# One core, pooled attention into a squared-ReLU layer into a soft mixture of experts: a later v pooling, a conversion step on another engine, and reloads in eight parts

## The chip, the cores and the metric

One core of a Trainium2 chip runs the whole program. The metric is the device time in microseconds (us) of one execution, the median of several. The kernel before takes 785.67 us (three runs, 785.44 to 789.61). A difference of about 0.5% (4 us) is what a measurement of this kernel can tell from no change.

The engines are named as in the profile: PE is TensorE's matmul side and PEld its weight loads, DVE is VectorE, ACT is ScalarE, POOL is GpSimd, SP is the engine from whose queue (SPq) every DMA of this kernel is issued.

## The reference

All inputs are drawn in float64 or float32 and the output is float32 of 4608 x 512. Cut to what is computed:

```
# attention: 8 sequences, 8 heads, 576 tokens, head size 64; k and v are averaged over groups of 8 tokens
k_p = k.reshape(B, H, Sp, 8, D).mean(axis=3);  v_p = v.reshape(B, H, Sp, 8, D).mean(axis=3)
attn = softmax(q @ k_p^T / sqrt(D));  x = attn @ v_p            # as 4608 x 512
# layer: d_ff 2048
g = max(x @ w_in, 0) ** 2;  y = g @ w_out
# soft mixture: 8 experts, 4 slots each
logits = y @ phi
d = softmax over tokens(logits);  slot_input = d.T @ y
slot_out[e] = max(slot_input[e] @ w1[e], 0) @ w2[e]
out = softmax over slots(logits) @ slot_out
```

## The kernel before

The 4608 tokens are 36 tiles of 128 (`t` = 0 to 35). For each tile the attention steps (`att_qT` to `att_av`) give x as two parts, `xh` and `xl`, whose sum keeps float32 precision. The first layer runs in **units**: unit (t, j) multiplies the tile's x with quarter j of `w_in` (512 of the 2048 columns) in 12 matmuls on PE into one of two PSUM buffers `l1` (line 453). There are 144 units, numbered here 0 to 143 in the order in which they run; from unit 16 on they go by pairs of tiles, (4,0) (5,0) (4,1) (5,1) and so on. ACT takes the ReLU of a finished unit (`r`, line 466), and the square `g` is made by DVE (line 473) or ACT (line 475). For the units of tiles 0 to 5 ACT squares; from unit 24 on, the first of tile 6, six of eight squares are DVE's. A PSUM buffer is free for the unit after next only when the square that reads it is done. Each g (256 KB) is stored to `g_dram` (line 477).

`w_out` is never multiplied with g in full: `phi` is folded into it (`turn_wo`, `fold_phi`, `sum_a`), which gives a small matrix `a_sb`. Its four quarters are loaded as float64 (`load_w`, line 373, 4 x 512 KB each, into the two buffers st0 and st1 in turn) and turned into float32 in integer and float steps by `f32_steps`: one on ACT (line 342), three on DVE (344, 347, 351), one addition on the engine that is handed in or else on GpSimd (355), one on DVE (356). `conv_out` (line 405) calls this for each of 16 pieces, with no engine handed in.

For a pair of tiles the logits need g transposed: `reload_turned` reads 512 KB of it back from `g_dram` in a transposing pattern (line 506, into `turned` or `tmp`), DVE finishes the transpose in blocks (`g_T`, line 514), PE multiplies with `a_sb` (`logits`, line 539), then `log_T` (568 on), `d_T` (603) and `dg` (613) add the pair's softmax-weighted g to the slot inputs. `dg` needs g itself. For the late pairs (from tile 10 on) it is still in SBUF; for the five **early pairs** (t = 0, 2, 4, 6, 8) `reload_g` reads the pair's 2 MB back into one buffer `g_back` (tag st0, lines 493 to 499) with two DMAs of 1 MB.

k and v of each sequence b are loaded in four parts of 288 KB (line 150) into three buffers `kv` that k and v share, and pooled. For the third sequence (b = 2) k is pooled by PE (`pool_k`, line 164, then 171 on DVE and 174 on ACT) and v by four DVE reductions of two heads each (`pool_v_dve`, line 189). They are called v0 to v3 here. From b = 3 on GpSimd pools (lines 157 to 159).

Order: the loop over the units runs each unit in two halves, called **slots** (slot 2u and 2u+1), and `at(slot, fn, ...)` hangs further work on a slot; `pinned(name, fn, ...)` hangs it behind the last instruction that was noted under a name, for instance the last store. The framework then orders each engine's instructions by a timeline that it simulates, so a slot is a wish and not a place. Each engine, and SP's queue, works through its own order strictly: an instruction that waits holds up all behind it.

Of the kernel before, what the change touches and what calls it, by code (L numbers as in the profile page):

```python
# [8 lines left out]
F32 = mybir.dt.float32  # L9
# [8 lines left out]
def kernel(  # L18
# [12 lines left out]
    nc = tc.nc  # L31
# [8 lines left out]
    P = 128  # L40
# [3 lines left out]
    NQ = 4  # L44
    QF = DFF // NQ
# [17 lines left out]
    stp = ctx.enter_context(tc.tile_pool(name="stp", bufs=1))  # L63
# [10 lines left out]
    vpp = (kvp, a3)  # L74
# [12 lines left out]
    g_dram = [dram.tile([2, NQ, CPQ, P, P], F32, tag=f"g_dram{t}", name=f"g_dram{t}") for t in range(0, NT - 4, 2)]  # L87
# [243 lines left out]
    def to_f32(src, dst=None, eng=None):  # L331
        steps = f32_steps(src, dst, eng)
        for _ in range(3):
            dst = next(steps)
        return dst

    def f32_steps(src, dst=None, eng=None):
        hi, lo = src[:, :, 1], src[:, :, 0]
        val, mag, low = (tmp[:, (3 * n_conv[0] + i) % 8] for i in range(3))
        n_conv[0] += 1  # L340
        dst = mag if dst is None else dst
        nc.scalar.activation(out=val, in_=hi.bitcast(F32), func=AF.Copy, scale=2.0 ** -112)  # L342
        yield
        nc.vector.tensor_scalar(  # L344
            out=mag.bitcast(U32), in0=val.bitcast(U32), scalar1=3, scalar2=None, op0=ALU.logical_shift_left
        )
        nc.vector.tensor_scalar(
            out=low.bitcast(U32), in0=val.bitcast(U32), scalar1=3, scalar2=0x7F800000,
            op0=ALU.logical_shift_left, op1=ALU.bitwise_and,
        )  # L350
        nc.vector.scalar_tensor_tensor(  # L351
            out=low, in0=lo, scalar=2.0 ** -52, in1=low, op0=ALU.mult, op1=ALU.mult
        )
        yield
        (eng or nc.gpsimd).tensor_tensor(out=mag, in0=mag, in1=low, op=ALU.add)  # L355
        nc.vector.scalar_tensor_tensor(
            out=dst.bitcast(U32), in0=val.bitcast(U32), scalar=0x80000000, in1=mag.bitcast(U32),
            op0=ALU.bitwise_and, op1=ALU.bitwise_or,
        )
        yield dst  # L360
# [38 lines left out]
    wo_t = {}  # L399

    def conv_out(j, c):
        st = st_t["out", j]
        if c == 0:
            wo_t[j] = st.rearrange("p c d two -> p c (d two)").bitcast(F32)[:, :, :DM]
        to_f32(st[:, c], wo_t[j][:, c])

    def natural(x):
        return x.rearrange("p (a c f) -> p c a f", a=4, f=32)
# [31 lines left out]
    hp_t, g_t, gT_t, L_t, dT_t, d_t, sc_d = {}, {}, {}, {}, {}, {}, {}  # L440
# [39 lines left out]
            if t >= ND:  # L480
                g_t[t, j] = g

    xbuf, gT_at = [], {}
    gT_free = [1, 2, 3, 4, 5]

    def turned():
# [4 lines left out]
        return xbuf  # L491

    def reload_g(t):
        g = stp.tile([P, 2, NQ, QF], F32, tag="st0", name="g_back")
        for u in range(2):
            nc.sync.dma_start(
                out=g[:, u].rearrange("p j (c f) -> p (j c) f", f=P),
                in_=g_dram[t // 2][u].rearrange("j c p f -> p (j c) f"),
            )
            for j in range(NQ):  # L500
                g_t[t + u, j] = g[:, u, j]

    def reload_turned(t, j):
        i = gT_at[t, j] = gT_free.pop(0)
# [242 lines left out]
    def at(slot, fn, *a):  # L747
        ev.setdefault(slot, []).append((fn, a))
# [20 lines left out]
    def post(t, s0, o, step=4):  # L769
        for j in range(NQ):  # L770
            if t < ND:
                at(s0 + step * j + o[1], pinned, "logits", logits, t, j)
            else:
                at(s0 + step * j + o[1], logits, t, j)
        for j in range(NQ):
            at(s0 + step * j + o[0], pinned, "sq", g_T, t, j)
            at(s0 + step * j + o[2], pinned, "store", reload_turned, t, j)

    def post_end(t, s0, p):
        at(s0 + p[0], log_T, t)  # L780
        at(s0 + p[1], d_T, t)
        if ND <= t < NT - 8:
            at(s0 + p[2], behind_l1, dg, t)
        else:
            at(s0 + p[2], dg, t)
# [42 lines left out]
    for j in range(NQ):  # L828
        s0 = 26 + 12 * j
        at((17, 31, s0 - 8, s0 - 8)[j], load_w, "out", j)  # L830
        for c in range(CPQ):
            at(s0 + 3 * c, paced, conv_out, j, c)
        at(s0 + 13, store_wo, j)
        for kk in range(KD):
            at(s0 + 14 + kk, behind_l1, turn_wo, j, kk)
        at(s0 + 22, behind_l1, fold_phi, j)
        at(s0 + 25, behind_l1, sum_a, j)
# [11 lines left out]
    for t in (NT - 4, NT - 2):  # L849
        s0 = SLOTS * t  # L850
# [12 lines left out]
    at(266, lambda: behind([("w1", 0, 1)], load_tail, 2))  # L863
    for t in range(0, ND, 2):
        s0 = 96 + 28 * (t // 2)
        at(s0 - 5, reload_g, t)
        post(t, s0, (3, 6, -2), 4)
        post_end(t, s0, (20, 21, 23))
    for b in range(1, B):
        s0 = a_at[b * S // P]  # L870
        for i in range(NPAIR):
            at(s0 - 16 + 2 * i, load_kv, k, raw_k, b, i)
            if b in PEP:
                at(s0 - 12 + 2 * i, pool_k, b, i)
            else:
                at(s0 - 12 + 2 * i, pool_kv, nc.gpsimd, raw_k, kp_t, b, i, kvp, "kp")
            at(s0 - 10 + 2 * i, load_kv, v, raw_v, b, i)
            if b in PEP:
                at(s0 - 4 + 2 * i, pool_v_dve, b, i, vpp[b % 2])
            else:  # L880
                at(s0 - 4 + 2 * i, pool_kv, nc.gpsimd, raw_v, vp_t, b, i, vpp[b % 2], "vp")
        if b not in PEP:
            at(s0 - 4, make_kb, b)
# [269 lines left out]
```

## Time and profile before

| | us |
|---|---|
| median of three runs | 785.67 |
| profiled execution, its own time | 786.77 |
| its span, first to last instruction | 785.0 |
| PE busy in the span | 732.8 (93%) |
| DVE busy | 517.2 (66%) |
| ACT busy | 392.7 (50%) |
| POOL busy | 149.1 (19%) |
| mean granted TensorE clock | 0.969 of full |

All times below are microseconds from the span's start in that execution. The units of the first layer run from 35 to 700; before that inputs arrive and are pooled, after it the experts and the output follow. The granted clock is a share of full speed: 1.00 is the 2.4 GHz level, 0.50 the 1.2 GHz one.

### The profile page before, as it was taken

To read this page: it belongs to the slowest core of one execution; us is meant where nothing else is said; L and a number is where in the kernel's file an instruction comes from. 1 tells how busy PE (TensorE), PEld (TensorE's weight loads), DVE (VectorE), ACT (ScalarE), POOL (GpSimd) and SP (SyncE) were. 2 spreads that over 40 slices of the span, in tenths; PEclk is the share of its full clock that TensorE was granted. 3 is DMA by queue.
4 is the path that set the end of the run, shared out by engine and by line. 5 is a ranking of instruction groups with operands and counts; after the bars stand their busy time and mean duration, and the time that the engine had idled before them with its cause. 6 is when DMAs were issued, how large, how long until landed. Compare 5 with 4: busy or idle time off the path is not lost.

```text
span 785.0 us, 14474 instructions
## 1 busy us (share of the span) xinstructions
PE 732.8 (93%) x5260; PEld 514.5 (66%) x5260; DVE 517.2 (66%) x1033; ACT 392.7 (50%) x1135; POOL 149.1 (19%) x167
## 2 busy tenths in 40 slices
PE   8789999979899999998999997989998999998993
PEld 7667787767677767575667664656665766663462
DVE  2996855485736678788868857868796765324253
ACT  2675677444547464444736551637385444332142
POOL 2232311164633500171022301320000000000000
PEclk7799999989999999999999999999999999999997
DMA  8955854758585884995696678769576325979998
GB/s 263 307 162 169 250 148 134 226 156 261 132 264 149 249 230 142 281 277 135 185 295 195 181 224 253 199 215 239 156 211 231 121 81 219 416 254 333 374 310 296
DMA packets 208296, 175.11 MB, mean 223 GB/s; under 512 B 74592, under 2 KB 165728, under 8 KB 208224
## 3 DMA queue, kind: packets, MB, share of 16 engines
q1 hardware_dynamic: 208224, 174.17, 72.2%
q8 instruction: 42, 0.69, 0.4%
q14 instruction: 30, 0.25, 0.1%
HBM read 126.94 MB, written 47.19 MB: 222 GB/s over the span
## 4 chain that ended last, share of the span: by engine, by line
PE 64%; DMA 10%; DVE 10%; ACT 5%; SPq 4%; POOL 3%; issue 2%; ACTq 0%; POOLq 0%; DVEq 0%
PE l L453 38%; PE misc L613 3%; PE pl L539 3%; DMA kv<-in_v_dram 2%; PE misc L1074 2%; DMA kv<-in_k_dram 2%; ACT aT L284 2%; PE l L1042 2%; PE gT L311 2%; PE gT L234 2%; DMA tmp<-g_dram 2%; PE att L234 2%; POOL kv L157 2%; PE att L311 2%; SPq L131 1%
## 5 line engine op out<-in xcount | busy, mean ns | idle before, releaser
L453 PE MATMUL l<-w,xh 128*128 128x512 f32 x1152 | 386.7, 415 | 10.1 <-DVE g L473 5.4
L453 PEld LDWEIGHTS l<-w,xh 128*128 128x128 f32 x1152 | 210.4, 192 | 85.3 <-issue 20.1
L453 PE MATMUL l<-w,xl 128*128 128x512 f32 x576 | 231.3, 402 | 0.0
L466 ACT ACTIVATE r<-l 128x512 f32<-128x512 f32 x144 | 86.6, 602 | 177.9 <-PE l L453 166.5
L453 PEld LDWEIGHTS l<-w,xl 128*128 128x128 f32 x576 | 110.0, 191 | 28.8 <-issue 3.5
L284 ACT COPY aT<-turned 32x256 f32<-32x256 f32 (+1 forms) x168 | 67.8, 403 | 23.3 <-DVE turned L293 19.7
L157 POOL TENSOR_TENSOR kv<-kv 72x512 f32<-72x512 f32 x40 | 55.0, 1379 | 125.7 <-DMA kv<-in_v_dram 78.8
L473 DVE TENSOR_TENSOR g<-l,r 128x512 f32<-128x512 f32 x57 | 38.8, 681 | 27.1 <-ACT r L466 21.0
L514 DVE STREAM_TRANSPOSE turned<-turned 128x1024 f32<-128x1024 f32 x39 | 47.5, 1227 | 10.8 <-DMA turned<-g_dram 10.8
L245 ACT ACTIVATE es<-gT,mx 128x72 f32<-128x72 f32 x120 | 36.8, 328 | 21.6 <-DVE mx L241 21.6
L245 ACT ACTIVATE es<-att,mx 128x72 f32<-128x72 f32 x120 | 37.0, 336 | 8.1 <-DVE mx L241 7.9
L286 DVE COPY aT<-turned 32x256 f32<-32x256 f32 (+1 forms) x120 | 37.2, 310 | 1.7 <-PE gT L311 0.2
L396 POOL TENSOR_TENSOR w<-tmp,w 128x512 fp32r<-128x512 f32 x16 | 22.8, 1430 | 70.1 <-ACT w L395 61.9
L473 DVE TENSOR_TENSOR tmp<-l,r 128x512 f32<-128x512 f32 x33 | 22.5, 682 | 18.7 <-ACT r L466 10.7
L475 ACT ACTIVATE g<-r 128x512 f32<-128x512 f32 x54 | 34.3, 636 | 0.9
L514 DVE STREAM_TRANSPOSE tmp<-tmp 128x1024 f32<-128x1024 f32 x25 | 30.4, 1226 | 6.2 <-DMA tmp<-g_dram 6.2
L355 POOL TENSOR_TENSOR tmp<-tmp 128x512 f32<-128x512 f32 x16 | 20.5, 1283 | 59.1 <-DVE tmp L351 59.1
L158 POOL TENSOR_TENSOR kv<-kv 72x256 f32<-72x256 f32 x40 | 30.6, 774 | 0.8
L613 PE MATMUL misc<-g,d 128*32 128x512 f32 x134 | 25.1, 620 | 5.1 <-DVE d L603 4.2
L268 DVE TENSOR_TENSOR es<-es,rs 128x576 f32<-128x576 f32 x36 | 28.8, 799 | 0.8
L344 DVE TENSOR_SCALAR tmp<-tmp 128x512 uint32<-128x512 uint32 x32 | 15.6, 488 | 19.8 <-ACT tmp L342 19.8
L159 POOL TENSOR_TENSOR kp<-kv 72x128 f32<-72x128 f32 x20 | 9.4, 484 | 100.6 <-PE att L204 100.6
(195 smaller groups left out, 1094.5 us busy)
## 6 DMA issues: line engine op xcount, KB each, us to landing
g_dram<-g SPq DMA_DIRECT2D x95, 256.0 KB
turned<-g_dram SPq DMA_DIRECT2D x39, 512.0 KB
w<-in_moe_w_dram SPq DMA_DIRECT2D x32, 512.0 KB
tmp<-g_dram SPq DMA_DIRECT2D x25, 512.0 KB
w<-in_moe_w_dram SPq DMA_DIRECT2D x6, 2048.0 KB
kv<-in_k_dram SPq DMA_DIRECT2D x32, 288.0 KB
kv<-in_v_dram SPq DMA_DIRECT2D x32, 288.0 KB
out_dram<-o SPq DMA_DIRECT2D x36, 256.0 KB
```

Source lines behind the costliest of these rows:

```text
L157: eng.tensor_tensor(out=x[:, :, 0:4], in0=x[:, :, 0:4], in1=x[:, :, 4:8], op=ALU.add)
L234: mark["sc", t] = nc.tensor.matmul(sc[off:off + n, i * 2 * SP:(i + 1) * 2 * SP], qT[:, pi, off:off + n], kb[b % 2][:, pi].rearrange("p a s ...
L245: mark["es", t] = nc.scalar.activation(out=es[:, e], in_=sv[:, h], func=AF.Exp, bias=mx[:, e:e + 1], accum_out=rsum[:, t % 8, e, 0:1],)
L284: nc.scalar.copy(out=dst, in_=src)
L286: eng[e].tensor_copy(dst, src)
L311: nc.tensor.matmul(px[e * D:(e + 1) * D, i * P + off:i * P + off + n], vp_t[b][:, 2 * i + e], aT[:, 2 * i + e, off:off + n],)
L453: mm = mark["l1", t, j] = nc.tensor.matmul(hp_t[t, j], steps[i][0], steps[i][1], start=(i == 0), stop=(i == 2 * n - 1))
L466: nc.scalar.activation(out=r, in_=hp, func=AF.Relu, scale=1.0 / (R * R if sq == "V" else R))
L473: mark["sq"] = nc.vector.tensor_tensor(out=dst, in0=pre, in1=src, op=ALU.mult)
L475: nc.scalar.activation(out=dst, in_=src, func=AF.Square)
L514: nc.vector.transpose(out=gc.rearrange("p (n i) -> p n i", i=32), in_=gc.rearrange("p (n f) -> p n f", f=32))
L613: mark["dg"] = nc.tensor.matmul(dp[32 * j:32 * j + 32], d[:, u], g if t < NT - 4 else natural(g), start=(u == 0), stop=(u == width(t) - 1),)
```

## The change

Three edits. The conversion of `w_out` is handed `nc.vector`, so its addition (line 355) goes from GpSimd to DVE, 16 times. The reload of an early pair's g is cut into eight DMAs of 256 KB, each behind the last store, one every three slots from three slots ahead of the pair's first slot to 18 slots behind it; the buffer is claimed one slot before. The DVE pooling of v is asked for `2 * b - 2` slots later: nothing for b = 1, two slots for b = 2.

```diff
-        to_f32(st[:, c], wo_t[j][:, c])
+        to_f32(st[:, c], wo_t[j][:, c], nc.vector)
...
     def reload_g(t):
-        g = stp.tile([P, 2, NQ, QF], F32, tag="st0", name="g_back")
+        g_back[t] = stp.tile([P, 2, NQ, QF], F32, tag="st0", name="g_back")
         for u in range(2):
-            nc.sync.dma_start(
-                out=g[:, u].rearrange("p j (c f) -> p (j c) f", f=P),
-                in_=g_dram[t // 2][u].rearrange("j c p f -> p (j c) f"),
-            )
             for j in range(NQ):
-                g_t[t + u, j] = g[:, u, j]
+                g_t[t + u, j] = g_back[t][:, u, j]
+
+    def reload_part(t, u, j):
+        nc.sync.dma_start(
+            out=g_back[t][:, u, j].rearrange("p (c f) -> p c f", f=P),
+            in_=g_dram[t // 2][u, j].rearrange("c p f -> p c f"),
+        )
...
         s0 = 96 + 28 * (t // 2)
-        at(s0 - 5, reload_g, t)
+        at(s0 - 4, reload_g, t)
+        for n in range(2 * NQ):
+            at(s0 - 3 + 3 * n, pinned, "store", reload_part, t, n // NQ, n % NQ)
...
             if b in PEP:
-                at(s0 - 4 + 2 * i, pool_v_dve, b, i, vpp[b % 2])
+                at(s0 - 4 + 2 * b - 2 + 2 * i, pool_v_dve, b, i, vpp[b % 2])
```

The order that comes out is the same up to unit 19. It differs at three places that matter here; line numbers of the changed kernel are up to four higher.

**Place A**, SP's queue around unit 22. `kv<-in_v` are the loads of v0 to v3, `st<-in_moe_w_out` is the third quarter of `w_out`. Before:

```order
L150 DMA kv<-in_v_dram 72x2x512
L150 DMA kv<-in_k_dram 72x2x512
L150 DMA kv<-in_v_dram 72x2x512
L477 DMA g_dram_105<-g 128x4x128
L373 DMA st<-in_moe_w_out_dram 128x1024 x4
L477 DMA g_dram_105<-g 128x4x128
L150 DMA kv<-in_v_dram 72x2x512 x2
L150 DMA kv<-in_k_dram 72x2x512
```

The same stretch of SP's queue in the changed kernel:

```order
L150 DMA kv<-in_v_dram 72x2x512
L150 DMA kv<-in_k_dram 72x2x512
L373 DMA st<-in_moe_w_out_dram 128x1024 x4
L477 DMA g_dram_105<-g 128x4x128
L150 DMA kv<-in_v_dram 72x2x512
L477 DMA g_dram_105<-g 128x4x128
L150 DMA kv<-in_v_dram 72x2x512
L477 DMA g_dram_105<-g 128x4x128
```

The 2 MB of `w_out` now stand ahead of the loads of v1, v2 and v3 (the last follows right behind these rows), where v1 was ahead of them.

DVE at the same place, from the reduction of v0 to the first square of tile 6 (`g<-l_1589`, unit 24). Before:

```order
L189 TENSOR_REDUCE vp<-kv 72x128
L319 TENSOR_TENSOR xl<-att,xh 128x512
L189 TENSOR_REDUCE vp<-kv 72x128
L171 TENSOR_SCALAR kb_119<-att 64x72 x2
L344 TENSOR_SCALAR tmp<-tmp 128x512
L347 TENSOR_SCALAR tmp<-tmp 128x512
L351 SCALAR_TENSOR_TENSOR tmp<-st,tmp 128x512
L428 COPY at_sb<-misc 128x4x4x32
L189 TENSOR_REDUCE vp<-kv 72x128
L356 SCALAR_TENSOR_TENSOR st<-tmp 128x512
L189 TENSOR_REDUCE vp<-kv 72x128
L473 TENSOR_TENSOR g<-l_1589,r 128x512
```

DVE there in the changed kernel, where unit 24 reads `l_1587`:

```order
L319 TENSOR_TENSOR xl<-att,xh 128x512
L171 TENSOR_SCALAR kb_119<-att 64x72
L344 TENSOR_SCALAR tmp<-tmp 128x512
L347 TENSOR_SCALAR tmp<-tmp 128x512
L171 TENSOR_SCALAR kb_119<-att 64x72
L189 TENSOR_REDUCE vp<-kv 72x128
L351 SCALAR_TENSOR_TENSOR tmp<-st,tmp 128x512
L189 TENSOR_REDUCE vp<-kv 72x128
L428 COPY at_sb<-misc 128x4x4x32
L355 TENSOR_TENSOR tmp<-tmp 128x512
L189 TENSOR_REDUCE vp<-kv 72x128
L473 TENSOR_TENSOR g<-l_1587,r 128x512
```

v1's reduction went behind the two `kb` rows and two conversion steps, v2's behind line 351; all four still stand ahead of unit 24's square, and the addition of line 355 is now among them.

**Place D**, DVE around the squares of units 33 and 34 (`l_2006` and `l_2077`). Before:

```order
L473 TENSOR_TENSOR g<-l_2006,r 128x512
L266 TENSOR_REDUCE rs<-rsum 128x8
L267 RECIPROCAL rs<-rs 128x8
L266 TENSOR_REDUCE rs<-rsum 128x8
L268 TENSOR_TENSOR es_121<-es_121,rs 128x576
L267 RECIPROCAL rs<-rs 128x8
L356 SCALAR_TENSOR_TENSOR st<-tmp 128x512
L268 TENSOR_TENSOR es_122<-es_122,rs 128x576
L473 TENSOR_TENSOR g<-l_2077,r 128x512
```

And in the changed kernel:

```order
L473 TENSOR_TENSOR g<-l_2006,r 128x512
L355 TENSOR_TENSOR tmp<-tmp 128x512
L266 TENSOR_REDUCE rs<-rsum 128x8 x2
L356 SCALAR_TENSOR_TENSOR st<-tmp 128x512
L267 RECIPROCAL rs<-rs 128x8 x2
L268 TENSOR_TENSOR es_121<-es_121,rs 128x576
L268 TENSOR_TENSOR es_122<-es_122,rs 128x576
L473 TENSOR_TENSOR g<-l_2077,r 128x512
```

Line 355 is now DVE's own, directly ahead of line 356 that needs it.

**Place F**, SP's queue around unit 93, where the reload of pair 6 begins (`g_dram_106` holds pair 6, `g_dram_114` the pair being computed, tiles 22 and 23). Before:

```order
L131 DMA qt<-in_q_dram 32x8x32 x2
L496 DMA g_back<-g_dram_106 128x16x128 x2
L477 DMA g_dram_114<-g 128x4x128
L506 DMA turned<-g_dram_114 128x2x512
L506 DMA tmp<-g_dram_106 128x2x512
```

In the changed kernel:

```order
L131 DMA qt<-in_q_dram 32x8x32 x2
L500 DMA g_back<-g_dram_106 128x4x128 x2
L477 DMA g_dram_114<-g 128x4x128
L508 DMA turned<-g_dram_114 128x2x512
L508 DMA tmp<-g_dram_106 128x2x512
```

Ahead of the same two transposing loads stand 512 KB of the reload where 2 MB stood; the other six parts follow one by one behind later stores. In this way pair 0's reload, which stood behind the 36th store, now begins behind the 47th; each pair's last part stands behind store 57, 71, 85, 99 and 113, and its `dg` follows unit 61, 75, 90, 103 and 116. Elsewhere the order of PE, DVE and ACT differs mostly around units 66 to 71, 95 to 100 and, most of all, 108 to 119.

## Rows read from the trace of the kernel before

**Rows 1.** Windows (us): length, each engine's busy (x instructions), PEclk, DMA share, GB/s.

```profile
60.00:700.00 640.00, 618.88 (x4031) 437.53 (x4030) 439.76 (x871) 336.46 (x993) 133.90 (x143) 0.99 0.69 208
...
157.40:160.85 3.45, 0.02 (x1) 0.00 (x1) 3.45 (x5) 0.00 (x0) 2.25 (x2) 0.86 0.73 205
160.85:166.80 5.95, 5.95 (x14) 4.69 (x15) 4.25 (x8) 3.01 (x17) 5.07 (x6) 0.51 0.92 292
...
474.30:477.30 3.00, 3.00 (x13) 1.82 (x14) 2.06 (x3) 0.00 (x0) 0.73 (x1) 0.50 1.08 350
...
209.00:212.00 3.00, 1.08 (x10) 0.81 (x9) 2.65 (x3) 2.46 (x5) 1.79 (x3) 1.00 0.28 44
```

**Rows 2.** One step of the chain of waits: start, us, what.

```profile
327.13 2.84 PE l L453 x12
```

**Rows 3.** Waits of PE, 60 to 700: us in total, times, longest.

```profile
PE l L453 <- DVE g L473: 5.4, 2, 3.4
PE misc L613 <- DVE d L603: 4.2, 4, 2.3
PE pl L539 <- DVE turned L514: 3.5, 1, 3.5
...
PE gT L299 <- ACT wt L420: 1.0, 1, 1.0
```

**Rows 4.** Timeline at place A: start, us, instruction [idle before <-releaser].

```profile
144.74 1.91 SPq L373 DMA_DIRECT2D st<-in_moe_w_out_dram  x4
...
147.27 1.98 DVE L189 TENSOR_REDUCE vp<-kv 72x128 f32<-72x1024 f32 x1 [2.83 <-DMA kv<-in_v_dram]
...
147.50 2.10 SPq L150 DMA_DIRECT2D kv<-in_v_dram  x2
...
155.89 1.91 DVE L189 TENSOR_REDUCE vp<-kv 72x128 f32<-72x1024 f32 x1 [2.79 <-DMA kv<-in_v_dram]
...
160.13 0.67 DVE L473 TENSOR_TENSOR g<-l,r 128x512 f32<-128x512 f32 x1
...
160.85 1.22 PE L453 MATMUL l<-w,xh 128*128 128x512 f32 x2 [3.43 <-DVE g L473]
```

**Rows 5.** SP's queue just ahead of that stretch, timeline.

```profile
140.22 0.33 SPq L150 DMA_DIRECT2D kv<-in_k_dram  x1
```

**Rows 6.** Line groups, whole span: busy us, mean ns of one | idle before, releaser.

```profile
L355 POOL TENSOR_TENSOR tmp<-tmp 128x512 f32<-128x512 f32 x16 | 20.5, 1283 | 59.1 <-DVE tmp L351 59.1
...
L356 DVE SCALAR_TENSOR_TENSOR st<-tmp 128x512 uint32<-128x512 uint32 x16 | 13.4, 834 | 11.2 <-POOL tmp L355 11.0
...
L355 DVE TENSOR_TENSOR tmp<-tmp 128x512 f32<-128x512 f32 x16 | 11.4, 719 | 0.1
```

**Rows 7.** Timeline at place D.

```profile
204.94 0.68 DVE L473 TENSOR_TENSOR g<-l,r 128x512 f32<-128x512 f32 x1
...
206.17 0.76 DVE L268 TENSOR_TENSOR es<-es,rs 128x576 f32<-128x576 f32 x1
...
209.35 1.20 DVE L356 SCALAR_TENSOR_TENSOR st<-tmp 128x512 uint32<-128x512 uint32 x1 [2.31 <-POOL tmp L355]
...
211.54 1.07 PE L299 MATMUL att<-ident,es 128*72 128x128 f32 x8 [1.92 <-DVE es L268]
```

**Rows 8.** Timeline at place F.

```profile
461.04 2.46 SPq L496 DMA_DIRECT2D g_back<-g_dram  x2
...
466.69 2.17 SPq L506 DMA_DIRECT2D turned<-g_dram  x1
...
472.94 1.25 DVE L514 STREAM_TRANSPOSE turned<-turned 128x1024 f32<-128x1024 f32 x1 [8.08 <-DMA turned<-g_dram]
```

**Rows 9.** Timeline at place E (unit 70).

```profile
347.22 1.25 DVE L514 STREAM_TRANSPOSE tmp<-tmp 128x1024 f32<-128x1024 f32 x1 [1.53 <-DMA tmp<-g_dram]
...
358.28 1.22 PE L453 MATMUL l<-w,xh 128*128 128x512 f32 x2 [1.63 <-DVE tmp L473]
```

**Rows 10.** Windows of 20 us over the new place of pair 0's reload, columns as in rows 1.

```profile
280.00:300.00 20.00, 19.85 (x141) 13.21 (x140) 17.33 (x37) 11.24 (x25) 0.00 (x0) 1.00 0.79 218
```

More of the change, by code (lines that the diff above doesn't have):

```diff
@@ L481, in l1_half @@
                 g_t[t, j] = g
-    xbuf, gT_at = [], {}
+    xbuf, gT_at, g_back = [], {}, {}
     gT_free = [1, 2, 3, 4, 5]
```

## Prediction, made before the changed kernel ran

> **What bounds the kernel now.** I read the busy shares first, then PE by windows, then PE's list of waits, and last the timeline around each wait. From 60 to 700 us, where the units run, PE is busy 618.9 of 640 us [rows 1]. So PE sets the pace and a change can win only what PE loses there: 21.1 us of idle time, plus the time at the lower clock. After some of the longer gaps the granted clock falls to the 1.2 GHz level. Behind the gap at 157.4 it is 0.51 for 5.95 us, behind the one at 470.8 it is 0.50 for 3.0 us [rows 1]. In the first, PE got through 14 records of the first layer; a run of 12 takes 2.84 us at full clock in the chain of waits [rows 2], so the 14 are worth 3.3 us and 2.7 us were lost. In the second half of 3.0 us, 1.5 us, is lost. Around 209 us, with a gap of 1.92 us, the clock stays at 1.00 [rows 1, 7]. So a gap that shrinks below that may give back more than its own length.
>
> PE's waits [rows 3] name five places. The largest total, 5.4 us behind DVE's square, is place A (3.43 us, before unit 26) and one of 1.93 us before unit 35, place C. Then come 4.2 us of `dg` waiting for `d_T`, 3.5 us at place F, 1.9 us at place D, 1.0 us at place B (171 us, ACT's copy `wt`). Place E is 1.63 us before unit 70 [rows 9].
>
> **Part 1, v pooled later: place A.** DVE stands still twice for v loads, 2.83 and 2.79 us [rows 4]. Behind it waits unit 24's square, which starts at 160.13; unit 26 needs its buffer at 157.4 and so PE idles 3.43 us. The wait is long because the v2 load, issued at 147.5 [rows 4], stands behind the 2 MB of `w_out` issued from 144.74 on: from there to v2's landing (155.9) are 11.15 us.
>
> The edit asks for two slots, but the four reductions still stand ahead of unit 24's square. What moves is small: v1's reduction goes behind the two `kb` rows and two conversion steps. The larger move is on SP: `w_out` goes ahead of v1. It no longer waits behind v1, whose buffer comes free only when DVE has pooled v0, so it can be issued right after the last k load (140.22) [rows 5], about 140.6 in place of 144.74. Then v1 is the load that lands late: 140.6 + 11.15, less about 1.4 us since v1 and a store (0.55 MB) no longer stand ahead of `w_out` (at the 400 GB/s that 2 MB in 5.2 us make; I estimate this from the load's four landings), so 150.3. From v1's landing DVE has three reductions (1.98 + 1.91 + 1.9), lines 351 and 428 (0.7 each), the added line 355 (0.72) and the square (0.68) [rows 4, 6]: 8.6 us, so the square ends at 158.9 where it ended at 160.8. The gap is 1.5 us in place of 3.43: 1.9 us won, and at that length I expect the clock to stay up, 2.7 us more. **4.6 us.** Ends: -0.7 (nothing lands sooner and DVE has one addition more) and 6.1 (v1 lands by 148.8; gap and low clock gone).
>
> **Part 2, `w_out` converted without GpSimd: places B, C, D.** Removed: 16 additions of 1.28 us on POOL, and DVE's wait for them, 11.0 us [rows 6]. Added: 16 additions on DVE; the same operation on the first weights takes 0.72 us there [rows 6], together 11.5 us. DVE's account is thus even (+0.5 us), what changes is where the time falls. At place D DVE waited 2.31 us because GpSimd pooled k and v first [rows 7]. Now, from the square's end at 205.62: line 355 0.72, two sums 0.3, line 356 0.83, two reciprocals 0.4, two normalisations 1.52 [rows 7] (the sums and reciprocals are estimates, a fifth of a normalisation each), end at 209.4. PE wants the second one at 209.6 and got it at 211.5, so **1.9 us** go. At place B ACT's copy `wt` now stands ahead of two exponentials where it stood behind them, **1.0 us**. At place C the addition stands ahead of unit 33's square in place of a wait of 0.45 us: 0, between -0.7 and 1.9. Elsewhere from 100 to 150 us PE has no gap and ACT squares, so that the added 0.72 us hide behind PE; if that cover is thin they cost up to 2 us. Sum **2.9 us**, ends -2.7 and 4.8.
>
> **Part 3, the reload in eight parts: places F and E.** At F two reload DMAs (2 MB) are issued from 461.04; the store behind them and the transposing load at 466.69 are held, the load arrives at 472.9 and DVE has waited 8.08 us [rows 8], PE 3.5. With 512 KB there, 1.5 MB less are ahead; at the 350 GB/s of that stretch [rows 1] this is 4.3 us, more than the 3.5. The gap goes and the lower clock behind it: 3.5 + 1.5 = **5.0 us**. At E the DVE waited 1.53 us for such a load, held by the same congestion 20 us after pair 2's reload, and two attention steps now stand ahead of that transpose; of 1.63 us and as much low clock again I take **1.5 us** (0 to 3.1).
>
> Costs. SP issues 40 DMAs for 10, but a part is of a store's kind and size: about 0.4 us each, eight as long as the two it replaces (2.46 us) [rows 8]. The last part of each pair stands four units (three for the last pair) ahead of its `dg`; a unit is over 4 us, a transfer at F took 6.3, so `dg` finds it landed. Pair 0's reload moves from the quiet stretch at 214 to about 258 to 300, where the DMA engines are 79% busy in the last 20 us [rows 10] but PE hardly waits: 0, at worst 2 us.
>
> The Trainium skill's page "DMA: Bandwidth & Descriptors" (Bandwidth, Measured) speaks against this part: its rule is to batch DMAs to at least 1 MiB for 75% of peak or more, with a fixed cost of about 2 us each. By that, pieces of 256 KB would add some 30 x 2 = 60 us of transfer time in all, and where it delayed a transposing load the sum would turn. The trace speaks for overlap: in the stretch at 474.3, with pieces of 256 to 512 KB in flight, 350 GB/s moved [rows 1].
>
> **Part 4, what the new order brings by itself.** PE, DVE and ACT are reordered around units 95 to 119, most at 108 to 119, where no gap but `dg`'s stood. A new gap there is priced like A or F, 5 to 6 us with its low clock, or like D, 1.9. The other way, `dg`'s 4.2 us could shrink. I charge **3.5 us**, ends -4 (a gain) and 8.
>
> **Sum.** 4.6 + 2.9 + 5.0 + 1.5 - 3.5 = 10.5 us. Against the profiled execution's own 786.8 us that is 776.3; the median is 785.7, 1.1 us lower, so the median goes to 775.2; I say **775**. The tail after 700 us has the same order and starts when PE's units end, so it moves along whole.
>
> **Rivals.**
>
> *A stays.* `w_out` ahead of v1 only exchanges which v is late, and unit 24's square still ends near 160.8. For it: the four reductions did not leave their place. Against it: SP can issue `w_out` 4 us sooner. Price: the 4.6 us of part 1; 780.
>
> *The change gives back what it takes.* The scheduler's order fits its own timeline and not the chip's; two gaps with low clock open at units 108 to 119, 2 x 5.5 = 11 us, where 3.5 were charged. For it: PE is at 97% and every reordering here meets an engine that is late by less than 2 us. Against it: the gaps removed have named causes. 775 + 7.5 = 782.7, up to 789.
>
> *The parts get in the way (slower).* They stand among the transposing loads of the pair being computed over some ten units of each of five pairs, and each delays what follows by its transfer, 0.75 us at 350 GB/s; with the fixed cost of the skill's rule it would be more. If that makes one gap like F's (5.0 us) in each pair, there are five instead of one: +20 against the sum without part 3 (10.5 - 6.5 = 4.0 won), 785.7 - 4 + 25 - 5 = 802; with half of the pairs hit about 793. It decides from the point where a transposing load lands later than PE's use; at E and F it did, with 1 to 2 MB ahead. Against it: a part is an eighth of that.
>
> **How the numbers follow.** Forecast, 770 to 781: 0.55. More than that (E, the `dg` waits and their clock go too), 765 to 770: 0.10. A stays, 777 to 782: 0.12. Gives back, 781 to 789: 0.14. Slower, 790 to 802: 0.09. For 8 in 10 I take 767 to 785. Within 0.5% is 781.7 to 789.6, about what a measurement can tell from no change. Faster gets the forecast, the upper case and nearly all of "A stays": 0.76; same 0.15; slower 0.09.
>
> **What would show it.** In the changed profile: DVE's wait for v ends before 152 and unit 26 starts within 1.5 us of PE's last matmul, with the clock at 1.00 up to 170; no wait of DVE for POOL at line 356 and no gap before the transposes at unit 36; the transposing load behind pair 6's first two parts under 5 us, no gap at unit 95; `g_back` never waited for. Wrong if the low-clock stretches behind A and F are still there, if PE's waits at units 108 to 119 exceed 6 us together, or if DVE's waits for `turned` and `tmp` loads grow.

## The result, and the profile after

The changed kernel takes 778.27 us (median of six, 774.76 to 779.99), the kernel before 787.37 us beside it (six runs). The ratio is 0.986, with a 95% interval of 0.9825 to 0.9894: 11.0 us faster (8.3 to 13.8). The two medians alone stand 9.1 us apart (0.988), which lies inside that interval. The sum had said 10.5 us, and 775 against the median of 785.67 that was known then. A second comparison of the same kernel gave 0.986 again (0.9823 to 0.9897).

The profiled execution took 778.38 us (span 776.6). Its line of PE's busy time, and the windows that answer to [rows 1] (length, busy us of PE, PEld, DVE, ACT and POOL, granted clock, DMA share, GB/s):

```profile
PE 729.7 (94%) x5260; PEld 513.8 (66%) x5260; DVE 530.4 (68%) x1049; ACT 391.8 (50%) x1135; POOL 130.7 (17%) x151
...
60.00:700.00 640.00, 621.96 (x4150) 440.17 (x4150) 457.92 (x908) 339.58 (x1005) 115.62 (x127) 0.99 0.72 212
156.70:160.30 3.60, 1.14 (x9) 0.97 (x8) 3.60 (x5) 0.60 (x1) 1.39 (x2) 0.88 0.27 82
160.30:166.30 6.00, 6.00 (x14) 4.74 (x15) 5.90 (x13) 2.94 (x17) 6.00 (x5) 0.50 0.94 311
```

POOL lost its 16 additions, DVE has 13 us more. Place A still has its gap, and behind it the clock is still at the 1.2 GHz level. PE's waits from 60 to 700 us (total, times, longest), against [rows 3]:

```profile
PE l L453 <- DVE g L473: 5.0, 3, 2.7
PE misc L615 <- DVE d L605: 4.4, 5, 1.3
PE l L453 <- DVE tmp L473: 1.5, 3, 0.6
PE misc L615 <- DVE lt_sb L585: 1.5, 1, 1.5
PE l L453 <- ACT r L466: 1.1, 1, 1.1
PE att L299 <- DVE es L268: 1.1, 1, 1.1
```

The 3.5 us for `turned` (place F) are gone; the wait for the square, 5.4 us before, is hardly smaller; `lt_sb` (unit 104) and ACT's ReLU (unit 116) stand where the list of before had other names.

Where the time went is best seen in stretches, each the time from the first matmul of one unit to that of another in the profiled execution (us). The last columns are runs that are told below.

| units | holds | before | changed | changed, 2nd run | second edit alone | third edit alone |
|---|---|---|---|---|---|---|
| 16 to 28 | A, B | 60.3 | 58.2 | 57.2 | 57.0 | 60.7 |
| 28 to 36 | C, D | 39.7 | 39.6 | 39.1 | 38.2 | 39.7 |
| 36 to 66 | | 127.7 | 127.4 | 127.4 | 127.3 | 127.4 |
| 66 to 76 | E | 48.6 | 46.0 | 45.7 | 47.5 | 47.6 |
| 76 to 92 | | 70.3 | 70.7 | 71.4 | 71.0 | 70.6 |
| 92 to 97 | F | 28.2 | 23.3 | 22.0 | 28.4 | 22.3 |
| 97 to 121 | | 115.3 | 116.0 | 115.4 | 115.3 | 115.5 |
| 121 to 143 | | 94.1 | 94.1 | 94.1 | 94.1 | 94.1 |

A column is one execution of several. That of the second edit alone took 778.78 us, where this kernel's median is 786.67, and that of the changed kernel's second run 774.65, where the median is 777.12: these two columns show a better case than the usual one.

With the same order of instructions a stretch still differs from one execution to the next: 97 to 121 took 115.3 us in the kernel before, with the clock at 0.50 for 3.4 us of it, and 113.7 in the run with the first edit alone, where it stayed at 1.00; 92 to 97 took 23.3 and 22.0 in the two executions of the changed kernel, with the clock at 1.00 in both. F is the clear gain (4.9 and 6.2 us), E the next (2.6 and 2.9), A to D gave 2.2 and 3.7 us.

### The profile page after: what moved, and what is told of

Read it like the earlier page. It is cut to its first block, busy times and chain, and to the rows that moved or that the text cites. A ratio compares the mean times of both kernels' runs of the same rounds, so it can differ in the third digit from the quotient of the medians.

```text
span 776.6 us, 14468 instructions
## 1 busy us (share of the span) xinstructions
PE 729.7 (94%) x5260; PEld 513.8 (66%) x5260; DVE 530.4 (68%) x1049; ACT 391.8 (50%) x1135; POOL 130.7 (17%) x151
## 4 chain that ended last, share of the span: by engine, by line
PE 62%; DVE 14%; DMA 14%; ACT 4%; issue 3%; SPq 2%; POOL 1%; DVEq 0%; ACTq 0%; POOLq 0%
PE l L453 37%; DMA g_dram<-tmp 4%; PE misc L615 3%; DMA kv<-in_v_dram 2%; PE pl L541 2%; DMA tmp<-g_dram 2%; PE misc L1078 2%; PE l L1046 2%; PE att L164 2%; PE gT L311 2%; PE att L311 2%; PE att L234 2%; DMA out_dram<-o 1%; ACT es L245 1%; PE gT L234 1%
## 5 line engine op out<-in xcount | busy, mean ns | idle before, releaser
L516 DVE STREAM_TRANSPOSE turned<-turned 128x1024 f32<-128x1024 f32 x39 | 47.6, 1230 | 8.1 <-DMA turned<-g_dram 8.0
L396 POOL TENSOR_TENSOR w<-tmp,w 128x512 fp32r<-128x512 f32 x16 | 22.7, 1421 | 70.6 <-ACT w L395 62.4
L158 POOL TENSOR_TENSOR kv<-kv 72x256 f32<-72x256 f32 x40 | 32.8, 825 | 0.8
L342 ACT ACTIVATE tmp<-st 128x512 f32<-128x512 f32 x32 | 21.5, 674 | 12.6 <-DMA st<-in_moe_w_in_dram 8.5
L245 ACT ACTIVATION_READ_ACCUMULATOR es<-att,mx 128x1 f32 x120 | 26.5, 221 | 0.0
```

Source lines behind the costliest of these rows:

```text
L158: eng.tensor_tensor(out=x[:, :, 0:2], in0=x[:, :, 0:2], in1=x[:, :, 2:4], op=ALU.add)
L245: mark["es", t] = nc.scalar.activation(out=es[:, e], in_=sv[:, h], func=AF.Exp, bias=mx[:, e:e + 1], accum_out=rsum[:, t % 8, e, 0:1],)
L516: nc.vector.transpose(out=gc.rearrange("p (n i) -> p n i", i=32), in_=gc.rearrange("p (n f) -> p n f", f=32))
```

## Experiments

### The first edit alone

```diff
-                at(s0 - 4 + 2 * i, pool_v_dve, b, i, vpp[b % 2])
+                at(s0 - 4 + 2 * b - 2 + 2 * i, pool_v_dve, b, i, vpp[b % 2])
```

> The kernel before with the first edit alone: the pooling of v of the third sequence asked for two slots later. Theory: the edit moves nothing, since the order of all five engines and of SP's queue comes out word for word as before; 785 to 790 us, ratio 1.000 within 0.004, a gap of about 3.4 us before unit 26 with the granted clock at half behind it. Rival, the prediction's part 1 (4.6 us won by this edit at place A): about 781, ratio 0.994, gap 1.5 us, clock full.

Measured: ratio 1.0021 (0.9989 to 1.0053), no difference. PE's row before unit 26 (start, us, instruction, idle before and what ended it):

```profile
162.31 1.16 PE L453 MATMUL l<-w,xh 128*128 128x512 f32 x2 [3.59 <-DVE g L473]
```

The gap is that of [rows 4]. The slot is a wish: in this run's trace the order of all five engines and of SP's queue is that of the kernel before, row by row. The run with the second edit alone, told next, lacks the first edit too, and has the changed kernel's order on every engine up to SP's first reload (211 us). The first edit is worth nothing.

### The second edit alone, the third edit alone

```diff
-        to_f32(st[:, c], wo_t[j][:, c])
+        to_f32(st[:, c], wo_t[j][:, c], nc.vector)
```

> The kernel before with the second edit alone: the addition of w_out's conversion on DVE. Theory: it is this edit that puts the w_out load ahead of the load of v1, and everything up to unit 45 comes from it; in the changed kernel unit 36 starts 1.9 us sooner than before, so this run is 2 us faster, ratio 0.9975 (0.994 to 1.000): gaps of about 0.5 and 1.9 us at place A, none at B, 2.7 at C, 1.1 at D, and E, F as before (1.6 and 3.5 us with half clock behind both). Rival, the prediction's parts 1 and 2 together: 7.5 us, ratio 0.9905.

Measured: 0.9954 (0.9925 to 0.9984), 3.6 us (1.3 to 5.9). So the move of `w_out` ahead of v1 in SP's queue belongs to this edit. In its profiled execution PE waited at A and, a little later, at B; the windows are the gap at A and what follows it:

```profile
155.76 0.73 PE L453 MATMUL l<-w,xh 128*128 128x512 f32 x2 [1.46 <-DVE g L473]
...
166.02 0.63 PE L299 MATMUL gT<-ident,es 128*72 128x128 f32 x4 [2.11 <-ACT wt L420]
```

```profile
155.80:162.00 6.20, 6.20 (x33) 5.29 (x34) 6.10 (x13) 3.57 (x18) 6.20 (x5) 1.00 0.95 307
```

Here the clock stayed at 1.00 behind A, and yet units 16 to 28 took 57.0 us, only 1.2 less than in the changed kernel's first profile, where it fell to 0.50 for 6 us and B had no gap. What full clock gave back at A, PE lost again at B, waiting for the copy `wt`. The changed kernel's second run shows the same (clock 1.00, then 2.1 us at B). B had been expected without a gap, which only the changed kernel's first profile bears out.

The third edit alone is `reload_g` and `reload_part` as in the change.

> The kernel before with the third edit alone: the reload in eight parts. Theory: the rest of the gain, about 6.5 us, ratio 0.992 (0.988 to 0.995): places A to D as before (3.4, 1.0, 1.9, 1.9 us), E and F without a gap and without half clock (about 4 and 5 us won), of which about 2.5 us are given back as new waits of PE for the d that dg needs (units 76, 104) and before unit 116. Rival, the parts need the second edit's earlier timing: under 3 us, ratio above 0.996.

Measured: 0.9894 (0.9863 to 0.9925), 8.3 us (5.9 to 10.8). The two together, 12.0, agree with the 11.0 of the whole change. The third edit carries two thirds of it. In its profile E and F have no gap, and 1.33 us stand before the `dg` of unit 75.

The forecast put the gap at E down to DVE's wait of 1.53 us for a transposing load [rows 9]. In the changed kernel DVE waits 1.52 us for such a load there, and PE has no gap. What differs is a group of five copies (line 286) that DVE makes a little later. In the kernel before it took 4.35 us, beside GpSimd's additions of k and v:

```profile
350.43 4.35 DVE L286 COPY aT<-turned 32x256 f32<-32x256 f32 x5
...
353.30 1.33 POOL L157 TENSOR_TENSOR kv<-kv 72x512 f32<-72x512 f32 x1
```

In the changed kernel it took 1.47 us. Two parts of k, loaded from 344.8 and 348.6 before, are loaded from 370.5 and 371.4 in SP's new order, so GpSimd adds beside the five copies of the next tile instead, and PE waits behind those:

```profile
343.92 1.25 DVE L516 STREAM_TRANSPOSE turned<-turned 128x1024 f32<-128x1024 f32 x1 [1.52 <-DMA turned<-g_dram]
...
348.43 1.47 DVE L286 COPY aT<-turned 32x256 f32<-32x256 f32 x5
...
375.58 3.95 DVE L286 COPY aT<-turned 32x256 f32<-32x256 f32 x5
...
378.05 1.34 POOL L157 TENSOR_TENSOR kv<-kv 72x512 f32<-72x512 f32 x1
...
382.11 1.92 PE L615 MATMUL misc<-g_back,d 128*32 128x512 f32 x16 [1.33 <-DVE d L605]
```

The traces of all twelve runs agree. Where the first group stands beside GpSimd (2.98 to 4.83 us, five traces), PE has a gap of 1.1 to 1.6 us before unit 70; where it does not (1.47 us, seven traces), there is none. Where the later group does (3.02 to 4.03 us, eight traces), PE waits 0.7 to 1.3 us before that `dg`; where it does not (1.43 us, four traces), it does not wait. DVE's wait for the load is 1.1 us or more in all twelve. So E's gap and the new wait before `dg` are the two sides of one move, that of GpSimd's additions; no run moves these alone.

### What counts in the reload: the bytes ahead, or the size of a piece

Two kernels, otherwise the changed one. In the first the reload is two DMAs of 1 MB, twelve slots apart; in the second it is all eight parts at one slot:

```diff
-            at(s0 - 3 + 3 * n, pinned, "store", reload_part, t, n // NQ, n % NQ)
+            if n % NQ == 0:
+                at(s0 - 3 + 3 * n, pinned, "store", reload_half, t, n // NQ)
```

```diff
-            at(s0 - 3 + 3 * n, pinned, "store", reload_part, t, n // NQ, n % NQ)
+            at(s0 - 3, pinned, "store", reload_part, t, n // NQ, n % NQ)
```

> The changed kernel with the reload in two DMAs of 1 MB, twelve slots apart, in place of eight of 256 KB. At place F 1 MB then stands ahead of the same store and transposing load, where the kernel before had 2 MB and the changed kernel 512 KB. Theory (what counts is the bytes ahead of the transposing load): 1 MB at 350 GB/s is 2.9 us sooner than before, which leaves a gap of about 0.6 us of 3.5; units 92 to 97 in 23.3 to 24.5 us (before 28.2, changed 23.3). Rival (small pieces count): half the gain or less, 25.5 us or more. Ratio 0.986 to 0.989 by the theory, 0.990 or more by the rival.

> The changed kernel with all eight reload parts asked for at one slot, so that they stand as eight DMAs of 256 KB in a row, 2 MB again, ahead of the same store and transposing load at place F. Theory (bytes ahead): F comes back, units 92 to 97 in 27 to 29 us as before (28.2; changed 23.3), and some of place E, ratio 0.991 to 0.995. Rival (small pieces let the transposing load through between them): 23.3 to 24.5 us, ratio 0.986.

Measured: two halves 0.9964 (0.9929 to 0.9999), eight at once 1.0052 (1.0014 to 1.009), slower than before. At place F the rows of SP's reload and transposing load, and of DVE's transpose behind it, are, first for the changed kernel,

```profile
456.41 1.00 SPq L500 DMA_DIRECT2D g_back<-g_dram  x2
...
458.06 0.45 SPq L508 DMA_DIRECT2D turned<-g_dram  x1
...
464.35 1.25 DVE L516 STREAM_TRANSPOSE turned<-turned 128x1024 f32<-128x1024 f32 x1 [3.06 <-DMA turned<-g_dram]
```

then for the two halves,

```profile
461.96 0.68 SPq L500 DMA_DIRECT2D g_back<-g_dram  x1
...
464.31 0.94 SPq L514 DMA_DIRECT2D turned<-g_dram  x1
...
471.47 1.25 DVE L522 STREAM_TRANSPOSE turned<-turned 128x1024 f32<-128x1024 f32 x1 [5.84 <-DMA turned<-g_dram]
...
472.81 0.64 PE L547 MATMUL pl<-turned,a_sb 128*32 128x256 f32 x8 [2.56 <-DVE turned L522]
```

and for the eight at once:

```profile
469.89 5.08 SPq L500 DMA_DIRECT2D g_back<-g_dram  x8
...
477.76 0.66 SPq L508 DMA_DIRECT2D turned<-g_dram  x1
...
482.66 1.25 DVE L516 STREAM_TRANSPOSE turned<-turned 128x1024 f32<-128x1024 f32 x1 [9.00 <-DMA turned<-g_dram]
...
484.01 0.67 PE L541 MATMUL pl<-turned,a_sb 128*32 128x256 f32 x8 [4.36 <-DVE turned L516]
```

With the kernel before [rows 8] this makes a series:

| ahead of the load | from the first reload issue to DVE's transpose | DVE's wait | PE's gap | units 92 to 97 |
|---|---|---|---|---|
| 512 KB (2 x 256) | 7.9 | 3.06 | 0 | 23.3 |
| 1 MB (1 x 1024) | 9.5 | 5.84 | 2.56 | 26.2 |
| 2 MB (2 x 1024) | 11.9 | 8.08 | 3.5 | 28.2 |
| 2 MB (8 x 256) | 12.8 | 9.00 | 4.36 | 29.1 |

The load comes later with the bytes ahead of it, 1.6 us from 512 KB to 1 MB and 2.4 from 1 to 2 MB (334 and 439 GB/s, where 350 was taken). Other executions with the same DMAs ahead spread: 6.9 to 8.4 us for 512 KB (seven traces) and 11.4 to 12.6 for two DMAs of 1 MB (three). So small pieces do not help the load, and what six DMAs more cost, 0.2 to 1.4 us, is hardly beyond the spread. The delay stands in SP's queue, ahead of the load's own issue: the store in between takes SP 0.45, 1.47, 2.99 and 2.66 us, and the load is issued 1.65, 2.35, 5.65 and 7.87 us after the first reload DMA; from there it needs 6.3, 7.2, 6.2 and 4.9 us. The theory stands, but its figure for 1 MB (a gap of 0.6) did not: the load came 2.4 us sooner than with 2 MB, where 2.9 was said, and PE had reached the multiply 8.3 us after the reload's issue (470.25) where in the kernel before it took 9.8. So the rival's bound for the stretch (25.5) was passed without its mechanism. The whole time missed the expectation as well (0.996 for 0.986 to 0.989): of some 9 us more than in the changed kernel's units, F holds 2.9, units 97 to 121 2.0, where the clock was at 0.50 for 6.8 us and not at all in the changed kernel's execution, 66 to 92 1.8, and 2.6 stand at units 16 to 36, where the order is that of the changed kernel; why clock and waits differ there, the runs do not show.

The eight at once lose elsewhere too: units 36 to 66 take 133.1 us in place of 127.4 and 66 to 76 take 52.0 in place of 46.0, with E's gap back. Pair 0's eight parts now stand among transposing loads, where before they had a quiet stretch; SP's issue took 7.3 us, and DVE's waits for such loads behind it were up to 2 us:

```profile
261.69 7.34 SPq L500 DMA_DIRECT2D g_back<-g_dram  x8
...
275.63 1.25 DVE L516 STREAM_TRANSPOSE tmp<-tmp 128x1024 f32<-128x1024 f32 x1 [2.04 <-DMA tmp<-g_dram]
```

### Place A: why does the gap stay?

In the changed kernel DVE reads, from v1's load on (SP's rows first):

```profile
139.61 2.77 SPq L373 DMA_DIRECT2D st<-in_moe_w_out_dram  x4
...
143.85 0.32 SPq L150 DMA_DIRECT2D kv<-in_v_dram  x1
```

```profile
152.15 2.02 DVE L189 TENSOR_REDUCE vp<-kv 72x128 f32<-72x1024 f32 x1 [3.19 <-DMA kv<-in_v_dram]
154.09 0.68 DVE L351 SCALAR_TENSOR_TENSOR tmp<-st,tmp 128x512 f32<-128x512 uint32 x1
154.69 1.96 DVE L189 TENSOR_REDUCE vp<-kv 72x128 f32<-72x1024 f32 x1
156.57 0.68 DVE L428 COPY at_sb<-misc 128x512 f32<-128x512 f32 x1
157.16 0.68 DVE L355 TENSOR_TENSOR tmp<-tmp 128x512 f32<-128x512 f32 x1
157.76 1.89 DVE L189 TENSOR_REDUCE vp<-kv 72x128 f32<-72x1024 f32 x1
159.57 0.68 DVE L473 TENSOR_TENSOR g<-l,r 128x512 f32<-128x512 f32 x1
```

```profile
160.31 1.22 PE L453 MATMUL l<-w,xh 128*128 128x512 f32 x2 [1.93 <-DVE g L473]
```

Three experiments move one thing each. The w_out loads spread:

```diff
-        at((17, 31, s0 - 8, s0 - 8)[j], load_w, "out", j)
+        if j == 2:
+            for c in range(CPQ):
+                at(s0 - 9 + 3 * c, load_w, "out", j, c, c + 1)
+        else:
+            at((17, 31, s0 - 8, s0 - 8)[j], load_w, "out", j)
```

> The changed kernel with the four DMAs of w_out's third quarter asked for three slots apart; in SP's queue two of them then stand ahead of v1's load and two behind it, where all four stood ahead. Theory 1 (v1's late landing, 8.3 us behind 2 MB, sets the gap at A): with 1 MB less ahead v1 lands about 2.9 us sooner, near 149.2 in place of 152.1; the gap of 2.5 us in two pieces shrinks to 0 to 1.2 us, units 16 to 28 in 55 to 57 us in place of 58.2, ratio 0.982 to 0.985. Theory 2 (DVE's own work ahead of the square sets it): the conversion steps that now stand between the reductions wait for the later half, 16 to 28 stays at 58, ratio 0.986.

Measured: 0.9807 (0.9757 to 0.9858, four executions), an interval that overlaps the changed kernel's (0.9825 to 0.9894), so a gain is not shown. v1 landed 9.3 us after the first w_out issue in place of 12.5, as theory 1 had it, but v2 became late in its place and the square ended 11.3 us after v1's landing:

```profile
145.21 1.98 DVE L189 TENSOR_REDUCE vp<-kv 72x128 f32<-72x1024 f32 x1 [4.10 <-DMA kv<-in_v_dram]
...
150.96 1.97 DVE L189 TENSOR_REDUCE vp<-kv 72x128 f32<-72x1024 f32 x1 [1.63 <-DMA kv<-in_v_dram]
...
155.86 0.68 DVE L473 TENSOR_TENSOR g<-l,r 128x512 f32<-128x512 f32 x1
```

The gap stayed (1.10 and 1.34 us), units 16 to 28 took 58.0: theory 2's figure, though by the loads and not by the conversion. Next, the squares off DVE:

```diff
-            sq = "A" if t < 6 else "VVVAVAVV"[2 * j + t % 2]
+            sq = "A" if t < 6 or (t < 8 and j == 0) else "VVVAVAVV"[2 * j + t % 2]
```

> The changed kernel with the squares of units 24 and 25 on ACT in place of DVE. Theory: the gap that is left at place A (0.5 and 1.9 us, with half clock for 6.8 us behind it) is unit 24's square queued on DVE behind four v reductions; ACT is idle there from 157.4 to 162.5, so the square is done before PE needs the buffer. Gap gone (1.9 us) and the lower clock with it (3.4 us): 3 to 5 us below the changed kernel, ratio to the kernel before about 0.981 where the changed kernel has 0.986. Rival A: PE is then held by the scores of the same tile, whose maximum (mx on DVE) is behind the same reductions: the gap moves a few us on, ratio 0.985 to 0.987. Rival B: a smaller gap, clock still at half behind it: 0.983 to 0.985.

Measured: 0.9855 (0.9827 to 0.9883), the changed kernel's own. The gap before unit 26 is gone and three stand behind it:

```profile
164.19 0.66 PE L418 MATMUL gT<-ident,st 128*128 128x128 f32 x4 [1.09 <-ACT es L245]
...
167.45 0.60 PE L299 MATMUL gT<-ident,es 128*72 128x128 f32 x4 [1.20 <-DVE es L268]
...
170.11 0.79 PE L299 MATMUL gT<-ident,es 128*72 128x128 f32 x4 [1.83 <-ACT wt L420]
```

That is rival A in its effect: the tile's maxima are late on DVE. In this order the first of them, at 162.33, stands behind the last reduction and behind four steps of the conversion (159.36 to 162.41), one of which takes 1.67 us beside GpSimd (last section). Last, the reductions themselves off DVE:

```diff
-            if b in PEP:
+            if b in PEP and b < 2:
                 at(s0 - 4 + 2 * b - 2 + 2 * i, pool_v_dve, b, i, vpp[b % 2])
```

> The changed kernel with v of the third sequence pooled by GpSimd (three additions a part, as from the fourth sequence on) in place of the four DVE reductions. Theory: what is left at place A is DVE's own work, four reductions of 1.9 to 2.0 us behind late loads, ahead of unit 24's square and of the tile's maxima; GpSimd no longer converts w_out and is free there. Gap and half clock at A gone, units 16 to 28 in 54 to 56 us where the changed kernel took 58.2, ratio to the kernel before 0.980 to 0.983 where the changed kernel has 0.986. Rival: GpSimd needs about 3 us a part and the last v lands near 157, so v is pooled after 160 and PE waits at the tile's weighted sum instead: units 28 to 36 take 42 us or more in place of 39.6, ratio 0.985 to 0.988.

Measured: 773.4 us, 0.979 (0.9745 to 0.9835). From 140 to 170 us PE now loses 0.3 us:

```profile
140.00:170.00 30.00, 29.70 (x219) 23.32 (x218) 19.02 (x36) 17.09 (x57) 14.27 (x15) 1.00 0.73 221
```

Units 16 to 28 take 53.1 us in place of 58.2, more than was expected; 28 to 36 take 41.2 in place of 39.6, because PE meets place C with 2.95 us and a fallen clock. What bound A was DVE's queue as a whole, its work and its waits for loads, and GpSimd, which the second edit had freed, could take four reductions of it. This run takes both the reductions and the waits for v off DVE, so it does not say which of them weighs more.

One step further, unit 33's square on ACT as well:

```diff
-            sq = "A" if t < 6 else "VVVAVAVV"[2 * j + t % 2]
+            sq = "A" if t < 6 or (t, j) == (9, 0) else "VVVAVAVV"[2 * j + t % 2]
```

> The changed kernel with v of the third sequence pooled by GpSimd and the square of unit 33 on ACT in place of DVE. Theory: the gap before unit 35 (place C, 2.95 us in the run with GpSimd, half clock for 6.8 us behind it) is that square queued on DVE behind three conversion steps that wait for ACT's; on ACT it follows its own ReLU. Units 28 to 36 in 37 to 39 us in place of 41.2, the rest as in that run: ratio to the kernel before 0.973 to 0.977. Rival: the conversion steps and the maxima of the tile are as late as before and PE meets them a few us on, as when units 24 and 25 were squared on ACT: 40.5 us or more, ratio 0.978 to 0.981.

> The changed kernel unaltered, beside the run above on the same chip, as the measure of what that one adds: ratio to the kernel before 0.986 (0.983 to 0.989) by the first comparison, with the low clock at place A in most executions and gaps of about 0.5, 1.9, 2.7 and 1.1 us up to unit 36. If the sum of the two single parts (4.6 and 10.6 thousandths) holds, 0.985.

Measured on one chip: 0.980 (0.9758 to 0.9843) with both moves, 0.986 (0.9823 to 0.9897) for the changed kernel. Units 28 to 36 took 38.7 us, as expected, but the square's move added nothing to 0.979: its gap came back one step later, behind the tile's normalisation on DVE, with the clock at 0.50 for 3.4 us behind it, and units 28 to 66 together take 168.7 us where the run with v on GpSimd alone took 168.6:

```profile
200.72 0.60 PE L299 MATMUL gT<-ident,es 128*72 128x128 f32 x4 [4.16 <-DVE es L268]
```

The medians of the two kernels with v on GpSimd are 773.4 and 772.95 us, those of the changed kernel 778.27 and 777.12; the intervals of single ratios touch, so by one comparison alone the step is not beyond doubt, by two it is 0.5 to 0.7% both times.

## Why the prediction came out right, and where its steps were wrong

The total was right: 10.5 us forecast, 11.0 measured, inside the range. In part that is luck, since two groups of terms were off in opposite ways. Parts 1 and 2, which the runs show to be one edit's doing, were put at 7.5 us and gave 3.6 (1.3 to 5.9). Parts 3 and 4 were put at 6.5 - 3.5 = 3.0 and gave 8.3 (5.9 to 10.8).

**Part 1, 4.6 us, mis-sized and put down to the wrong edit.** It took the move of `w_out` in SP's queue for the v edit's; that edit moves nothing. The step on SP held (issue expected at 140.6, measured at 139.61) and so did DVE's 8.6 us from v1's landing to the end of the square (8.1). The landing was expected at 150.3 and came at 152.15: v1's load could be issued only at 143.85, when v0 was pooled, and landed 8.3 us later. The gap was 0.5 + 1.9 us instead of 1.5. The larger error was the clock's 2.7 us. At half clock PE was not alone late, DVE and ACT were too, as 58.2 us for units 16 to 28 against 57.2 and 57.0 suggest; where the clock stayed up, PE waited 2.1 us at B. A and B together gave 2.0 to 3.3 us in the three profiles where 5.6 were forecast: B's wait, said to go, was gone in one of them and 2.1 us in the other two. One of the prediction's own signs of being wrong, the low clock behind A, is there in the first profile and not in the second.

**Part 2, 2.9 us.** The mechanism held: line 356 waits 0.2 us where it had waited 11.2 [rows 6], as the line groups show:

```profile
L355 DVE TENSOR_TENSOR tmp<-tmp 128x512 f32<-128x512 f32 x32 | 23.6, 741 | 0.4
...
L356 DVE SCALAR_TENSOR_TENSOR st<-tmp 128x512 uint32<-128x512 uint32 x16 | 13.5, 844 | 0.2
```

The gain was smaller: C grew to 2.68 us and D shrank to 1.06, not to 0, in the changed kernel; units 28 to 36 take 39.6, 39.1 and 38.2 us in the three profiles for 39.7, where 1.9 less was forecast. The step that failed is "C: 0", an addition ahead of unit 33's square priced at the wait that it replaced. The low end of C (-0.7) was what happened.

**Part 3.** F was forecast at 5.0 and gave 4.9, by the bytes ahead, as the series shows; the load itself still took 6.3 us from its issue, where under 5 had been named as the sign, and what fell was the time until SP could issue it. E was put at 1.5 with 3.1 as its end; units 66 to 76 gained 2.6 us with a new gap of 1.33 us in them, so some 3.9 for E, more than its end. The step that failed is the wait itself: DVE's wait for the load stayed (1.53 and 1.52 us), and the 2.9 us that DVE's copies lost beside GpSimd went, a term that the forecast does not have. SP's issues took 0.5 us each (1.00 us for two) where 0.4 was said. The Trainium skill, page "DMA: Bandwidth & Descriptors" (Bandwidth, Measured), has the rule for batching to 1 MiB that the prediction weighed; its 2 us for each DMA are that page's figure for DMAs issued from GpSimd (Anatomy of one DMA), and these are issued from SP. The trace does not bear out the 60 us worked out from it: the same 2 MB in pieces of 256 KB came 0.9 us later, at most some 0.2 us for each DMA more.

**Part 4, -3.5 us, charged too much.** At units 97 to 121, reordered most, the changed kernel takes 116.0 us for 115.3: new gaps (1.1 us before unit 116) stand against the wait before unit 120, which fell from 2.3 us to 1.05 and 0.6 and lost its low clock (0.50 for 3.4 us before). The one clear loss is `dg` of pair 2, 1.33 us, because the softmax on DVE now comes later, behind the copies that GpSimd's additions stretch from 1.43 to 3.95 us; some 2 us in all. This loss and E's gain are one move, which the forecast counted in two parts and saw in neither.

**Rivals.** "A stays" is half true. "The change gives back what it takes" did not come: PE's waits at units 108 to 119 are 2.5 us together, with the clock at 1.00. "The parts get in the way" did not happen with the parts spread; DVE's waits for `turned` and `tmp` loads fell from 17.0 to 13.8 us. With the parts together the time is 792.9 us. That this is near the rival's 793 is chance: there 2 MB stand ahead of one load again, and not single parts among the loads.

## What to carry to other kernels

Look first whether a planner heeds an edit at all; one that leaves every engine's order as it was is worth nothing, whatever it asks for. Count the bytes that stand ahead of an urgent load in its queue and spread a bulk transfer over the stretch in which it has time: the size of its pieces matters little, their place much. When a gap is removed, price the next late thing behind it: at an engine with a late queue, moving one consumer moves the gap, moving work off that engine closes it. And compare how long the same rows take before and after: at E DVE's wait for its load stayed, and the length of five copies changed.

## What the runs showed of the hardware

The clock behind much the same gap fell in one execution and not in another: at A it was 0.50 for 6 us behind 0.5 and 1.9 us of idle time, and 1.00 behind 1.7 us in the second run of the same kernel:

```profile
158.40:164.00 5.60, 5.60 (x31) 4.79 (x31) 5.50 (x13) 3.46 (x18) 5.60 (x5) 1.00 0.97 319
```

Behind the 2.68 us at place C it stayed at 1.00 in the changed kernel. A sum should therefore carry the lower clock as a range and not as a sure term.

DVE's steps stretched where they started while GpSimd was adding. The five copies of place E are one case, a step of the conversion is another: line 351 took 0.68 us at 153.78 in the kernel with the squares on ACT, and 1.67 at 160.74 beside an addition of GpSimd that began at 160.17:

```profile
153.78 0.68 DVE L351 SCALAR_TENSOR_TENSOR tmp<-st,tmp 128x512 f32<-128x512 uint32 x1
...
160.74 1.67 DVE L351 SCALAR_TENSOR_TENSOR tmp<-st,tmp 128x512 f32<-128x512 uint32 x1
```

```profile
160.17 1.69 POOL L157 TENSOR_TENSOR kv<-kv 72x512 f32<-72x512 f32 x1 [1.49 <-DVE st L356]
```

The Trainium skill, page "SBUF — State Buffer" (SBUF: two separate sides), says that DVE and GpSimd share a pair of ports as an exclusive lock, for a DVE operation with two SBUF inputs among others; the rows agree, as GpSimd's addition ends at 161.86 and 0.55 us, most of an undisturbed step, are left of line 351. In the kernel before, 23 of its 32 steps of line 351 have no GpSimd operation beside them and took 0.63 to 0.69 us, six that began before one took 0.67 to 0.69, and three that began while one ran took 1.11 to 1.65. Work given to GpSimd is thus not free for DVE.
